# Three of each unit's 64 row maxima on ScalarE and GpSimd, in a fused attention and feed-forward kernel on one core

## The chip, the cores and the metric

The kernel runs on one core of one Trainium2 chip. The metric is the device time of one execution in microseconds (us), lower is better. Engines: TensorE (PE, and PEld for its weight loads), VectorE (DVE), ScalarE (ACT), GpSimd (POOL) and SyncE (SP, which here only issues DMAs). GpSimd issues DMAs too, in the order of its own program.

## The reference

One transformer block on x of shape 1 x 2048 x 512 in float32: a modulated layer norm, softmax attention with 32 heads of 16, and a SwiGLU feed-forward of width 1792.

```python
mod = (_silu(c) @ w_mod).reshape(c.shape[0], 6, 1, -1)
h = _layernorm(x) * (1 + ca) + sa
# in _A_ref: scores = q k^T / 4;  p = softmax(scores);  o = p v;  o @ wo
x = x + ga * _A_ref(h, A_wqkv, A_wo)
h = _layernorm(x) * (1 + cb) + sb
# in _B_ref: (silu(h @ w_gate) * (h @ w_up)) @ w_down
x = x + gb * _B_ref(h, B_w_gate, B_w_up, B_w_down)
```

## The kernel before, in words

**Units.** The attention is cut into 32 units: 4 chunks of 512 queries by 8 groups of 4 heads. A unit has 16 steps, one for each 128 keys. In a step TensorE makes four score tiles (`score`, L569), ScalarE takes their exponentials out of PSUM (L571), and `pv_step` multiplies them with the values (L584).

**Maxima.** The exponentials need each row's maximum over all 2048 keys, which is made ahead: `max_one(r)` multiplies 128 queries with 512 keys into a PSUM bank (L521), and VectorE reduces the 512 columns to one maximum a row (L523). A unit has 64 of them, four in a step, and they run LEAD = 21 steps ahead of the scores. When a unit's last one is issued, `max_rows` reduces the four maxima of a row to one (L528, VectorE), and the result is turned by TensorE (L533 to L535) and stored in two further rows of the unit's query tile `qop`, so that the score matmul subtracts it. The maxima use banks 0 to 3 in turn (`four`), the scores three others (`bank`).

**Order.** Everything is issued in an order written by hand; each engine follows its own part of it. `plain` runs windows of three pairs of one score and one maximum, and after each window one or two halves of a `pv_step`. The first `plain` stretch is 147 steps long (STARTS), attention alone; units 2 to 8 have their maxima in it. After it, feed-forward work of the finished chunk is mixed in.

**What else is in that stretch.** `split_weights` splits the feed-forward weights in two parts on GpSimd (L646, L647, L684) and stores them to DRAM (L650): three steps of it in each unit, about 3, 5 and 8 steps after a unit's scores begin. `close_unit(u)` runs when the values of unit u are done: the loads of the keys `kop` (three tiles in rotation) and queries `qop` for unit u + 3 (`load_k`, `load_q`; SP issues one half of the rows and GpSimd the other, L445), and, some steps later, the division: the denominators go to DRAM (L595, L600), come back broadcast as `rb` (L605), and GpSimd multiplies (`out_c`, L611) and stores (L612). In the order of GpSimd's program a unit of this stretch is so: loads for a coming unit, two weight steps, the multiplication at L611, the third weight step.

`tmp(name)` gives one of four 128 x 512 tiles in rotation, which the feed-forward uses too.

Of the kernel before, what the change touches and what calls it, by code (L numbers as in the profile page):

```python
# [14 lines left out]
ALU = mybir.AluOpType  # L15
AX = mybir.AxisListType
# [12 lines left out]
CW = S // NC  # L29
NG = H // 4  # L30
# [9 lines left out]
WIN = 3  # L40
HALVES = (2, 1, 1, 2)
ORDER = (0, 2, 1, 3)
UG = 16 * NG
PTS = 13
FBANKS = (3, 6)
# [56 lines left out]
def block_kernel(ctx, tc, x, wqkv, wo, w_gate, w_up, w_down, c, w_mod, out):  # L102
    nc = tc.nc
# [389 lines left out]
    qop, mx, pts, pv, o_, due, res = {}, {}, {}, {}, {}, {}, {}  # L493
# [12 lines left out]
    def load_q(u):  # L506
        ci, g = divmod(u, NG)
        qop[u] = pb.tile([P, 2, CW], F32R, name="qop", tag="qop", bufs=3)
        first, second = [(nc.gpsimd, nc.sync)[k] for k in ((0, 0), (1, 1), (1, 0))[min(u, 1) + (u > 2)]]
        load_parts(qop[u], qd, g, ci * CW, (ci + 1) * CW, second, first)  # L510

    def max_one(r):

        u, t = divmod(r // 4, 16)
        b, e = 1 - r % 4 // 2, r % 2
        s, qt, kc = t // 4 % 2, t % 4, t // 8 * 2 + e
        if u not in mx:
            mx[u] = pb.tile([P, 2, 2, 4, NC], F32, name="mx", tag="mx", bufs=3)
        rows = slice(64 * b, 64 * b + KR)
        pm = four("pm")  # L520
        nc.tensor.matmul(pm, qop[u][rows, s, qt * P:(qt + 1) * P], kop[u % 3][rows, s, kc * CW:(kc + 1) * CW],  # L521
                         start=True, stop=True)
        nc.vector.tensor_reduce(mx[u][:, b, s, qt, kc:kc + 1], pm, op=ALU.max, axis=AX.X)  # L523

    def max_rows(u):

# [36 lines left out]
    def score(i, h):  # L563
        u, kt = divmod(i, 16)
        rows = slice(64 * (h % 2), 64 * (h % 2) + KR + 2)
        p_ = pb.tile([P, CW], F32, name="pt_", tag="pt", bufs=PTS)
        pts.setdefault(i, {})[h] = p_
        sp = bank("st_")
        nc.tensor.matmul(sp, kop[u % 3][rows, h // 2, kt * P:(kt + 1) * P], qop[u][rows, h // 2, :],  # L569
                         start=True, stop=True)  # L570
        nc.scalar.activation(p_, sp, AF.Exp, scale=SCALE)  # L571
# [42 lines left out]
    def at(i, f):  # L614
        due.setdefault(i, []).append(f)
# [16 lines left out]
    def tmp(name):  # L632
        return pf.tile([P, CW], F32, name=name, tag="tmp", bufs=4)
# [261 lines left out]
    def begin(ci):  # L895
        x2 = pf.tile([P, 4, D], F32, name="x2", tag="x2", bufs=1)
        act = [pf.tile([P, NK, CW], F32R, name=f"act{a}", tag=f"act{a}", bufs=1) for a in range(2)]
        hT = [pf.tile([P, NK, CW], F32R, name=f"act{a}", tag=f"act{a}", bufs=1) for a in range(2)]
        chunks[ci] = ch = Chunk(ci, x2, act, hT)
        ch.load_x2(nc.sync if ci else nc.gpsimd)  # L900
# [43 lines left out]
    at(3, lambda: begin(0))  # L944
    at(UG - 2, lambda: chunks[0].load_wo())

# [3 lines left out]
    def after(i):  # L950
# [9 lines left out]
        if i == -2:  # L960
# [8 lines left out]
            load_q(2)  # L969
        if 0 <= i < UG and i % 16 in ((1, 4) if i < 16 else (3, 5, 8) if i < UG - 16 else (1, 3, 5)):  # L970
            next(weights2, None)
# [5 lines left out]
    def pair_of():  # L977
        nonlocal done
        i = done // 4 - 1
        most = 4 * n - 4 * (LEAD - 1)  # L980
        h = (ORDER if done < most else (0, 1, 2, 3))[done % 4]
        work = [lambda: score(i + 1, h)]
        if done < most:
            work.insert(1 - h % 2, lambda: max_one(done + 4 * (LEAD - 1)))
        for f in work:
            f()
        done += 1
        if side:
            side.pop(0)()

    for i in range(-LEAD, -1):
        if i == -LEAD + 3:
            load_k(1)
            load_q(1)
        for k, r in enumerate((0, 2, 1, 3)):
            max_one(4 * (i + LEAD) + r)
            if (4 * (i + LEAD) + k) % 6 == 1:
                take(late, 12 if i > -LEAD else 4)
        if i == -2:
            four, work = three, bank  # L1000
            for k in range(4):
                bank = Turn(7, 3, 6)
                for _ in range(WIN):
                    pair_of()
                bank = work
                if k < 3:
                    take(late, (9, 9, 8)[k])
        after(i)
        while side:
            side.pop(0)()  # L1010
# [174 lines left out]
```

## Time and profile before

| | |
|---|---|
| median of 3 runs | 1828.58 us (1827.91 to 1830.11) |
| span of the profiled execution | 1827.6 us |
| busy in that span | PE 99%, DVE 83%, ACT 69%, POOL 25% |
| the maxima on VectorE (L523) | 2048, 1274.3 us busy |
| chain that ended last | PE 82%, DVE 14% of the span |

The profile is of one execution of its own, whose time is its span; the runs are timed apart from it, and their median is 1.0 us over that span. Times in rows of order are microseconds from the span's start. In those rows stand the start, the duration, the engine, the line of the kernel, the operation, what it writes and reads, how often, and in brackets how long the engine had been idle and what ended that. A POOL or SP row with DMA in its name is the issue of a transfer, not the transfer.

### The profile page before, as it was taken

What the parts mean: (1) busy time and instruction counts of PE and PEld (TensorE: products, weight loads), DVE (VectorE), ACT (ScalarE), POOL (GpSimd) and SP (SyncE); (2) the same over time, 40 slices, a digit from 0 to 9 for tenths busy, and PEclk for the clock granted to TensorE, in tenths of its full rate; (3) what the DMA queues carried; (4) which work ended last, traced back from release to release, by engine and by line L of the source; (5) the groups of instructions that cost most, each with busy time, mean ns of one, the idle gap of its engine ahead of it and who ended that gap; (6) DMA issues with size and microseconds to landing.
All of it is one profiled execution on the core that took longest, in us unless ns stands there. A gap on an engine that the chain in (4) does not pass through costs nothing.

```text
span 1827.6 us, 41072 instructions
## 1 busy us (share of the span) xinstructions
PE 1818.3 (99%) x16904; PEld 1199.7 (66%) x16904; DVE 1523.2 (83%) x2554; ACT 1255.7 (69%) x2434; POOL 459.9 (25%) x538
## 2 busy tenths in 40 slices
PE   9999999999999999999999999999999999999999
PEld 7876444444455777776565777776464577767887
DVE  5578999999999888889999888889999988821544
ACT  4223888888888776777888777777888877774211
POOL 3612544556223111111123111111113011130200
PEclk9999999999999999999999999999999999999999
DMA  9884876667845454453544554444643536333742
GB/s 306 288 225 143 202 195 178 178 167 200 206 81 125 103 123 142 114 148 71 144 110 107 139 125 119 124 115 91 160 79 57 119 89 162 130 119 120 276 167 110
DMA packets 80488, 267.63 MB, mean 146 GB/s; under 512 B 19604, under 2 KB 24212, under 8 KB 59620
## 3 DMA queue, kind: packets, MB, share of 16 engines
q1 hardware_dynamic: 61324, 179.71, 34.1%
q0 software_dynamic: 18288, 84.49, 19.4%
q8 instruction: 133, 2.18, 0.5%
q10 hardware_dynamic: 688, 0.80, 0.2%
q14 instruction: 55, 0.45, 0.1%
HBM read 201.85 MB, written 62.13 MB: 144 GB/s over the span
## 4 chain that ended last, share of the span: by engine, by line
PE 82%; DVE 14%; ACT 1%; DMA 1%; issue 0%; SPq 0%; DVEq 0%; ACTq 0%
PE bank L584 21%; PE bank L786 20%; PE bank L569 14%; DVE mx L523 14%; PE bank L521 11%; PE bank L211 7%; PE bank L796 7%; DMA wm_ab<-in_w_mod 1%; PE bank L770 0%; DMA kop<-o_dr 0%; PE bank L163 0%; DMA rb<-d_dr 0%; ACT sq L820 0%; PE bank L839 0%; DVE v_flat L870 0%
## 5 line engine op out<-in xcount | busy, mean ns | idle before, releaser
L523 DVE TENSOR_REDUCE mx<-bank 128x1 f32<-128x512 f32 x2048 | 1274.3, 686 | 108.3 <-PE bank L521 54.6
L569 PE MATMUL bank<-qop,kop 50*128 50x512 f32 x2048 | 728.6, 425 | 0.4 <-ACT pt__16523 L571 0.2
L521 PE MATMUL bank<-kop,qop 48*128 48x512 f32 x2048 | 725.1, 425 | 0.3
L569 PEld LDWEIGHTS bank<-qop,kop 50*128 50x128 f32 x2048 | 343.6, 184 | 167.9 <-issue 49.7
L521 PEld LDWEIGHTS bank<-kop,qop 48*128 48x128 f32 x2048 | 344.0, 185 | 107.0 <-DVE mx L523 62.3
L786 PE MATMUL bank<-act,wgu 64*128 64x512 f32 x1872 | 301.4, 392 | 0.0
L786 PEld LDWEIGHTS bank<-act,wgu 64*128 64x128 f32 x1872 | 197.1, 187 | 24.3
L611 POOL TENSOR_TENSOR on<-o,rb 128x512 f32<-128x512 f32 x31 | 39.8, 1285 | 506.3 <-DMA rb<-d_dr 358.9
L786 PE MATMUL bank<-wd,mid 64*128 64x512 f32 x912 | 134.1, 397 | 0.1
L858 POOL CAST mid<-m 128x512 fp32r<-128x512 f32 x40 | 24.3, 607 | 380.9 <-DVE m L856 180.2
L786 PEld LDWEIGHTS bank<-wd,mid 64*128 64x128 f32 x912 | 88.3, 186 | 15.5 <-ACT first L893 3.2
L211 PE MATMUL bank<-hT,wqs 128*128 128x512 f32 x384 | 94.4, 397 | 0.4 <-DVE wqs L351 0.4
L854 DVE SCALAR_TENSOR_TENSOR q<-th,bank 128x512 f32<-128x512 f32 x56 | 38.2, 683 | 54.3 <-ACT th L850 54.3
L211 PEld LDWEIGHTS bank<-hT,wqs 128*128 128x128 f32 x384 | 70.7, 188 | 18.8 <-issue 2.9
L850 ACT ACTIVATE th<-bank 128x512 f32<-128x512 f32 x56 | 33.3, 594 | 57.9 <-PE bank L796 57.9
L870 DVE TENSOR_TENSOR x<-bank,x 128x512 f32<-128x512 f32 x84 | 53.9, 685 | 19.0 <-PE bank L786 16.8
L856 DVE TENSOR_TENSOR m<-bank,q 128x512 f32<-128x512 f32 x56 | 38.7, 692 | 21.7 <-PE bank L796 19.7
L859 POOL TENSOR_TENSOR mid<-m,mid 128x512 fp32r<-128x512 f32 x40 | 51.6, 1289 | 3.3
L796 PE MATMUL bank<-wd,mid 128*128 128x512 f32 x216 | 51.5, 394 | 0.0
L211 PE MATMUL bank<-wqs,hT 128*128 128x512 f32 x192 | 48.1, 398 | 0.0
L786 PE MATMUL bank<-wgu,act 64*128 64x512 f32 x288 | 47.0, 393 | 0.0
L796 PEld LDWEIGHTS bank<-wd,mid 128*128 128x128 f32 x216 | 40.4, 188 | 9.0 <-POOL mid L859 0.2
(6301 smaller groups left out, 5148.9 us busy)
## 6 DMA issues: line engine op xcount, KB each, us to landing
wgu<-gu_dr SPq DMA_DIRECT2D x48, 1024.0 KB
wd<-wd_dr SPq DMA_DIRECT2D x28, 1024.0 KB
kop<-kd SPq DMA_DIRECT2D x33, 768.0 KB
kop<-kd POOLq DMA_DIRECT2D x29, 768.0 KB, 8.7
gu_dr<-wgu POOLq DMA_DIRECT2D x14, 1024.0 KB, 13.6
kd<-prt SPq DMA_DIRECT2D x16, 512.0 KB
qd<-prt SPq DMA_DIRECT2D x16, 512.0 KB
kop<-gu_dr SPq DMA_DIRECT2D x8, 1024.0 KB
```

The lines of the kernel that those rows point to most:

```text
L211: nc.tensor.matmul(pt, lhs(a, k), rhs(b, k), start=(n == 0), stop=(n == 3 * nk - 1))
L521: nc.tensor.matmul(pm, qop[u][rows, s, qt * P:(qt + 1) * P], kop[u % 3][rows, s, kc * CW:(kc + 1) * CW], start=True, stop=True)
L523: nc.vector.tensor_reduce(mx[u][:, b, s, qt, kc:kc + 1], pm, op=ALU.max, axis=AX.X)
L569: nc.tensor.matmul(sp, kop[u % 3][rows, h // 2, kt * P:(kt + 1) * P], qop[u][rows, h // 2, :], start=True, stop=True)
L584: nc.tensor.matmul(pv[u][32 * h:32 * h + 32, cols], v_flat[:, e0:e0 + 32], p_[h][:, cols], start=(kt == 0 and half == 0), stop=(kt == 15), ...
L611: mul.tensor_mul(on, o, rb)
L786: nc.tensor.matmul(outs[e], lhs(e, a, k)[rows], rhs(b, k)[rows], start=(ph == 0 and j == 0), stop=(j == z and (ph == 1 or trade is not None)),
L796: nc.tensor.matmul(outs[e], lhs(e, a, k), rhs(b, k), start=(j == 0), stop=(j == z))
L854: nc.vector.scalar_tensor_tensor(q, th, 1.0, outs[0], op0=ALU.add, op1=ALU.mult)
L856: nc.vector.tensor_mul(m32, outs[1], q)
L859: (nc.gpsimd if slow else nc.vector).tensor_sub(mid[:, 1, :], m32, mid[:, 0, :].bitcast(F32))
L870: nc.vector.tensor_add(ch.x2[:, t, :], outs[e], ch.x2[:, t, :])
```

## The change

In units 2 to 8 the maxima number 0, 6 and 12 of the 64 are not reduced by VectorE. ScalarE copies their PSUM bank into a `tmp` tile ("far"), and after the third copy is issued, GpSimd takes the maxima: `max_apart` halves the width again and again, each time as b + max(a - b, 0) in three operations: each tile for itself down to 64 columns, the three together from there to two, and then the last pair. Its scratch is a fourth `tmp` tile ("near"). The results go where VectorE would have put them.

```diff
+APART = (0, 6, 12)
...
-        nc.vector.tensor_reduce(mx[u][:, b, s, qt, kc:kc + 1], pm, op=ALU.max, axis=AX.X)
+        place = mx[u][:, b, s, qt, kc:kc + 1]
+        if 2 <= u <= NG and r % 64 in APART:
+            apart.append((tmp("far"), place))
+            nc.scalar.copy(apart[-1][0], pm)
+            if len(apart) == len(APART):
+                max_apart()
+        else:
+            nc.vector.tensor_reduce(place, pm, op=ALU.max, axis=AX.X)
+
+    apart = []
+
+    def larger(out, a, b, d):
+        nc.gpsimd.tensor_sub(d, a, b)
+        nc.gpsimd.tensor_scalar_max(d, d, 0.0)
+        nc.gpsimd.tensor_add(out, b, d)
+
+    def max_apart():
+
+        k, w = len(apart), CW // 8
+        d = tmp("near")
+        few = d[:, CW // 2:CW // 2 + k * w].rearrange("p (k w) -> p k w", k=k)
+        for j, (far, _) in enumerate(apart):
+            for v in (4 * w, 2 * w, w):
+                larger(few[:, j, :] if v == w else far[:, 0:v], far[:, 0:v], far[:, v:2 * v], d[:, 0:v])
+        while w > 2:
+            w //= 2
+            larger(few[:, :, 0:w], few[:, :, 0:w], few[:, :, w:2 * w],
+                   d[:, 0:k * w].rearrange("p (k w) -> p k w", k=k))
+        nc.gpsimd.tensor_sub(d[:, 0:k], few[:, :, 0], few[:, :, 1])
+        nc.gpsimd.tensor_scalar_max(d[:, 0:k], d[:, 0:k], 0.0)
+        for j in range(k):
+            nc.gpsimd.tensor_add(apart.pop(0)[1], few[:, j, 1:2], d[:, j:j + 1])
```

## The prediction

> **What bounds the kernel now.** I read the page's first part, then the chain of work that ended last in the stretch where the changed units lie, then busy times by unit, then VectorE's and GpSimd's rows in order of time.
>
> ```profile
> span 1827.6 us, 41072 instructions
> PE 1818.3 (99%) x16904; PEld 1199.7 (66%) x16904; DVE 1523.2 (83%) x2554; ACT 1255.7 (69%) x2434; POOL 459.9 (25%) x538
> ...
> 242.63 26.92 DVE mx L523 x46
> ...
> core 0: us, PE busy (x) PEld busy (x) DVE busy (x) ACT busy (x) POOL busy (x), PEclk, DMA share, GB/s
> 242.00:280.00 38.00, 38.00 (x392) 18.42 (x390) 38.00 (x66) 33.26 (x66) 20.09 (x21) 1.00 0.72 188
> ...
> 242.42 0.22 DVE L528 TENSOR_REDUCE m<-mx 128x16 f32<-128x64 f32 x1
> 242.54 28.79 DVE L523 TENSOR_REDUCE mx<-bank 128x1 f32<-128x512 f32 x48
> ...
> 474.30 0.21 DVE L528 TENSOR_REDUCE m<-mx 128x16 f32<-128x64 f32 x1
> ```
>
> The reduction of L528 closes a unit's maxima, so its rows mark the units: unit 2's at 242.42 us, unit 8's at 474.30, six units of 38.65 us on average between them. The changed units 2 to 8 therefore lie between about 202 and 474 us. There the chain runs along VectorE's maxima (46 in a row), which follow each other every 0.60 us (48 in 28.79), without a gap. So VectorE paces this stretch; TensorE's queue is as full, ScalarE is at 88% and GpSimd at 53%. By these shares alone the change looks right: it takes work from the engine that paces to the one that is half idle.
>
> But GpSimd's half idle time is not free time of any kind: where in its order the new work lands decides. Its rows, first by unit, then around one place:
>
> ```profile
> 241.67 1.28 POOL L611 TENSOR_TENSOR on<-o,rb 128x512 f32<-128x512 f32 x1 [17.21 <-ACT pt__2307 L571]
> ...
> 282.55 1.27 POOL L611 TENSOR_TENSOR on<-o,rb 128x512 f32<-128x512 f32 x1 [18.48 <-DMA rb<-d_dr]
> ...
> 322.36 1.28 POOL L611 TENSOR_TENSOR on<-o,rb 128x512 f32<-128x512 f32 x1 [17.44 <-DMA rb<-d_dr]
> ...
> 360.23 1.26 POOL L611 TENSOR_TENSOR on<-o,rb 128x512 f32<-128x512 f32 x1 [15.24 <-DMA rb<-d_dr]
> ...
> 250.88 0.58 POOL L650 DMA_DIRECT2D wd_dr<-wd  x1 [0.30 <-POOL wd L647]
> 251.46 0.58 POOL L445 DMA_DIRECT2D kop<-kd  x1
> 252.03 0.58 POOL L445 DMA_DIRECT2D qop<-qd  x1
> ...
> 263.48 0.59 POOL L650 DMA_DIRECT2D gu_dr<-wgu  x1 [0.30 <-POOL wgu L647]
> ```
>
> All of GpSimd's idle time in a unit is one wait, at L611, for a row of denominators that comes when its unit ends. From one L611 to the next, without that wait, GpSimd needs 282.55 - 241.67 - 18.48 = 22.4 us (22.4 and 22.6 for the next two). Its slack is 38.65 - 22.4 = 16.2 us a unit. That is the number to hold against the change.
>
> **The change, part by part.** (1) VectorE loses 3 of 64 maxima in each of 7 units: 3 x 0.60 = 1.8 us a unit, 12.6 us in all, on the path as long as nothing else takes its place.
>
> (2) ScalarE gains 3 copies of 128x512 from PSUM a unit. The row of such a copy in this stretch:
>
> ```profile
> L588 ACT COPY o<-bank x6: 585/588/612, 214.8 to 408.3; 128x512 f32<-128x512 f32 x6
> ```
>
> That is 1.8 us a unit, against 4.7 us that ScalarE is idle in the 38 us of the table. They come within 13 of a unit's 64 steps, between the exponentials, and can hold a score bank some tenths of a us longer; between 0 and 1.8 us a unit. I take nothing, because they are covered if (3) is right; if it is wrong they eat part of (1).
>
> (3) GpSimd gains one call of `max_apart` a unit. Each of the three tiles goes through widths 256, 128 and 64 with three operations each (27), all three together through 32, 16, 8, 4 and 2, that is 96, 48, 24, 12 and 6 elements a partition (15), and then two operations and three adds (5): 47 instructions, nearly all waiting for the one before. The rows nearest to them:
>
> ```profile
> 565.11 0.20 POOL L753 TENSOR_TENSOR rs<-rs,mv 128x4 f32<-128x4 f32 x1
> 565.40 0.20 POOL L754 TENSOR_SCALAR rs<-rs 128x4 f32<-128x4 f32 x1
> ...
> 567.08 0.20 POOL L756 TENSOR_TENSOR rs<-mv,rs 128x4 f32<-128x4 f32 x1
> 567.38 0.77 POOL L765 TENSOR_SCALAR mid<-x,rs,rs 128x512 f32<-128x512 f32 x1
> ...
> L647 POOL TENSOR_TENSOR wgu<-mid,wgu 128x512 fp32r<-128x512 f32 x28 | 35.8, 1280 | 2.3
> L647 POOL TENSOR_TENSOR wd<-mid,wd 128x1024 fp32r<-128x1024 f32 x7 | 16.7, 2387 | 0.6
> L646 POOL CAST wgu<-mid 128x512 fp32r<-128x512 f32 x28 | 17.3, 618 | 0.0
> ```
>
> From 565.11 to 567.08 seven dependent operations of 4 elements take 1.97 us: 0.28 us each from start to start, though each lasts 0.20. The fixed part is 47 x 0.28 = 13.2 us. Two-input operations cost (2387 - 1280)/512 = 2.16 ns an element: 3 x 2 x 448 + 2 x 186 = 3060 elements, 6.6 us. One-input operations cost (772 - 197)/508 = 1.13 ns by L765 and L754 (0.8 by the cast): 3 x 448 + 186 = 1530 elements, 1.7 us. Less 0.3 us for the four elements that are in the fixed part: 21.2 us a call. This is 5 us over the slack of 16.2. The change spends most of GpSimd's time not on elements but on starting instructions.
>
> Here a rule bears on the row. The Trainium skill, Perfetto Trace Analysis, section GPSIMD Engine Instruction, holds that GpSimd spans don't add up and are to be timed by the spacing of consecutive starts. The spacing of 0.28 us against spans of 0.20 agrees with it. By spans alone the call would be 47 x 0.20 + 8.0 = 17.4 us, still over the slack.
>
> (4) What is queued behind it. In program order the call comes when the third tile is copied, at the unit's 13th maximum; that is after the weight step that ends with the store at 250.88 us, and before the load of the next unit's keys and queries at 251.46. Each queue: on POOL the load of `kop` and `qop` for unit u+1 (half the rows; SP issues the other half unmoved) stands behind the call for unit u. No transfer is added. How long these loads take, and when they are needed:
>
> ```profile
> kop<-kd POOLq DMA_DIRECT2D x1, 768.0 KB, 8.3
> ...
> kop<-kd POOLq DMA_DIRECT2D x1, 768.0 KB, 15.7
> ...
> qop<-qd POOLq DMA_DIRECT2D x1, 192.0 KB, 8.8
> ...
> 278.26 0.40 PE L521 MATMUL bank<-kop,qop 48*128 48x512 f32 x1
> ...
> 471.69 0.39 PE L521 MATMUL bank<-kop,qop 48*128 48x512 f32 x1
> ```
>
> The rows of 8.3 and 8.8 us are the load for unit 3, with nothing ahead of it in the queue (the load for unit 5, behind a 1 MB store, took 15.7; after 21 us of arithmetic that store has left). `qop` lands 0.57 + 8.8 = 9.4 us after the `kop` issue. The two matmuls are the first maxima of unit 4 (the 257th of L521) and of unit 9 (the 577th). They read the rows that POOL loads, and TensorE takes its work in order: if these are late, the exponentials and the values behind them are late too.
>
> A second rule, for the landing: the Trainium skill, DMA: Bandwidth & Descriptors, section on the SWDGE (gpsimd) path, gives 2.0 us and bytes over 436e3, an estimate of 3.8 us for 768 KB. The row has 8.3, so the measurement decides; by the rule the sum below would be 4.5 us less.
>
> **The sum.** The rows for the start and the end of the stretch:
>
> ```profile
> 203.02 0.60 POOL L650 DMA_DIRECT2D wo_dr<-wgu  x1 [0.30 <-POOL wgu L647]
> 211.65 0.57 POOL L445 DMA_DIRECT2D kop<-kd  x1 [8.03 <-PE bank L521]
> ...
> 223.87 0.59 POOL L650 DMA_DIRECT2D gu_dr<-wgu  x1 [0.30 <-POOL wgu L647]
> ...
> 507.00 1.28 POOL L611 TENSOR_TENSOR on<-o,rb 128x512 f32<-128x512 f32 x1 [23.89 <-ACT pt__5723 L571]
> ```
>
> Unit 2's call finds GpSimd idle (its wait of 8.0 us ends at 211.65), runs from 203.6 to 224.8, and its load lands at 234, before unit 3 starts near 240; the weight work (12.8 us, from 211.65 to the end of the store of 223.87) then ends before the L611 at 241.67. Covered. Unit 3's call starts at 251.46 and ends at 272.7; the load lands at 282.1 instead of serving at 278.26: 3.8 us late. From there GpSimd has no wait left: 12.6 us of weight work (251.46 to 264.07) bring it to 285, past 282.55 when the denominators come, and the next call follows. Its period is 22.4 + 21.2 = 43.6 us, against 38.65. The load for unit 9 then lands at 251.46 + 21.2 + 5 x 43.6 + 9.4 = 500.1, 28.4 us after 471.69. VectorE's relief is worth nothing in a stretch paced by GpSimd; at most unit 2's 1.8 us ahead of it would be kept, and I take none. Behind unit 8 there are no more calls, GpSimd gets its waits back (23.9 us at the L611 of 507.00) and the lateness stays as it is. 1827.6 + 28.4 = 1856.0 us of span; the median of the runs is 1.0 us over the profiled span, so 1857.0.
>
> Both ends of the unknown cost: 17.4 us a call (spans without the spacing) gives a period of 39.8 and 28.4 - 6 x 3.8 = 5.6 us, 1834; one-input operations at the worst row of that kind, below, 2.8 ns an element, give 23.8 us a call and 28.4 + 6 x 2.6 = 44 us, 1873. I stay at the chained rows, the nearest in kind.
>
> ```profile
> L265 POOL TENSOR_SCALAR minus<-ident 128x128 f32<-128x128 f32 x1 | 0.5, 548 | 0.1
> ```
>
> **The rivals.** (a) Faster: GpSimd keeps up and VectorE's relief counts. It decides at a call of 16.2 us or less, which would take 47 instructions at 0.17 us fixed; no row is that short. Then up to 12.6 us come off, but TensorE is also full and ScalarE's copies crowd the same 13 steps, so about half: 1822. Chance 0.07. (b) Nothing: the calls fit or nearly fit, and what VectorE gives up TensorE takes over as pace, which the full PE column speaks for and the spacing row against: 1828, chance 0.04. (c) Slower, but by ScalarE: the copies hold score banks and VectorE's reduction waits for GpSimd's result; 7 x 1.8 us at most, 1841, while GpSimd holds its loads in time. Nothing shows this stronger than (3); chance 0.04. (d) My forecast, 1857, chance 0.85; between its ends it may lie from 1834 to 1873.
>
> **How the numbers follow.** 0.2% of this kernel is 3.7 us, about what a measurement can tell from no change. Faster 0.07 from (a), same 0.04 from (b), slower 0.89 from (c) and (d). The range 1838 to 1870 leaves out (a) and (b), and the outer tips of (d), 2 in 10 together.
>
> **What would show it.** Right: no wait left at L611 from the second call on; POOL near full from 251 us on; the loads of L445 on POOL some 20 us later against the unit's start than now; a wait of TensorE for `kop` or `qop` of some 4 to 5 us once in each of units 4 to 9; L528 rows 43 to 44 us apart there and 38 before and after; VectorE with gaps. Wrong: a call much under 21 us, L611 still waiting, or L528 rows 36 to 38 us apart, which would be (a).

## The result: slower by 3.1%, and the profile after

| | before | after |
|---|---|---|
| median of the runs | 1829.25 us (4 runs, 1827.91 to 1830.11) | 1886.0 us (4 runs, 1883.17 to 1886.64) |
| ratio to before | | 1.0307 [1.0295, 1.0319] |
| span of the profiled execution | 1827.6 us | 1883.9 us |

The forecast was 1857.0 us, from 1838 to 1870: right in direction, 28.4 us expected and 56.3 us found between the two profiled spans. Where they arose is seen in the time at which each unit's first maximum reaches TensorE (rows of the line that multiplies for the maxima, L521 before and L522 after; us from the span's start):

| unit | 3 | 4 | 5 | 6 | 7 | 8 | 9 | 10 |
|---|---|---|---|---|---|---|---|---|
| before | 239.8 | 278.3 | 317.1 | 355.8 | 394.2 | 433.1 | 471.7 | 510.1 |
| after | 239.0 | 289.5 | 337.0 | 380.4 | 431.2 | 477.4 | 525.9 | 567.4 |
| late by | -0.8 | 11.2 | 19.9 | 24.6 | 37.0 | 44.3 | 54.2 | 57.3 |

Until unit 3 nothing is lost. From unit 4 on every unit is late by 5 to 12 us more, and after unit 10 it stays.

In the changed kernel the line numbers are shifted: L522 is the multiplication for a maximum, L531 VectorE's reduction, L536, L537 and L538 the subtraction, the max with 0 and the addition of a halving, L446 the loads of `kop` and `qop`, L637 the load of `rb`, L643 the multiplication that was L611. The page of the changed kernel, its first lines, the row of the granted clock in 40 slices, and the shares of the chain that ended last:

```profile
span 1883.9 us, 41445 instructions
PE 1834.6 (97%) x16904; PEld 1200.5 (64%) x16904; DVE 1516.4 (80%) x2533; ACT 1266.1 (67%) x2455; POOL 596.0 (32%) x867
...
PEclk9999998898989999999999999999999999999999
...
PE 85%; POOL 4%; DVE 4%; DMA 3%; ACT 2%; issue 1%; SPq 0%; POOLq 0%; DVEq 0%
```

Over the whole span GpSimd is busy only a third of the time, so the first part of the page alone would not convict it. But DVE's share of the chain has fallen from 14% to 4%, and POOL and DMA have 7% together, where everything beside PE and DVE had 4%. GpSimd's rows in order of time, changed kernel, in the first three changed units, then the two later waits for `rb` and the load for unit 9 (start, duration, engine, line, operation):

```profile
203.09 0.75 POOL L536 TENSOR_TENSOR near<-far 128x256 f32<-128x256 f32 x1
...
226.24 0.64 POOL L446 DMA_DIRECT2D kop<-kd  x1
...
246.59 1.29 POOL L643 TENSOR_TENSOR on<-o,rb 128x512 f32<-128x512 f32 x1 [7.57 <-ACT pt__2431 L603]
...
256.40 0.75 POOL L536 TENSOR_TENSOR near<-far 128x256 f32<-128x256 f32 x1
...
279.54 0.64 POOL L446 DMA_DIRECT2D kop<-kd  x1
280.18 0.58 POOL L446 DMA_DIRECT2D qop<-qd  x1
...
292.17 1.29 POOL L643 TENSOR_TENSOR on<-o,rb 128x512 f32<-128x512 f32 x1
...
325.17 0.64 POOL L446 DMA_DIRECT2D kop<-kd  x1
...
388.52 1.28 POOL L643 TENSOR_TENSOR on<-o,rb 128x512 f32<-128x512 f32 x1 [5.15 <-DMA rb<-d_dr]
...
483.44 1.26 POOL L643 TENSOR_TENSOR on<-o,rb 128x512 f32<-128x512 f32 x1 [3.76 <-DMA rb<-d_dr]
...
516.37 0.64 POOL L446 DMA_DIRECT2D kop<-kd  x1
```

A call lasts from the first row of L536 to the issue of `kop`: 226.24 - 203.09 = 23.15 us, 279.54 - 256.40 = 23.14. The load for unit 4 is issued at 279.54, where it was issued at 251.46 before, and unit 4 needed it at 278.26. Between 279.54 and 325.17 GpSimd has no wait worth a row: 45.6 us is its own program, one call in it. Two later periods hold a wait for `rb`, and the first L643 comes late (246.59, before 241.67).

What TensorE does meanwhile: the waits of the changed kernel, all engines, 200 to 560 us (total, times, longest), and two steps of the chain in the same stretch:

```profile
DVE mx L531 <- PE bank L522: 45.5, 18, 12.9
PE bank L522 <- DMA qop<-qd: 37.7, 5, 11.0
...
POOL on L643 <- DMA rb<-d_dr: 8.9, 2, 5.1
```

```profile
280.18 9.14 DMA qop<-qd
...
325.80 11.08 DMA qop<-qd
```

TensorE, in whose order the unit's first maximum comes next, stands still for the query rows, five times in 37.7 us, and VectorE behind it. VectorE's own rows in order of time, changed kernel, show that it has nothing to do then, and that while it has work it is as fast as before:

```profile
279.76 0.22 DVE L560 TENSOR_REDUCE m<-mx 128x16 f32<-128x64 f32 x1
292.88 3.08 DVE L531 TENSOR_REDUCE mx<-bank 128x1 f32<-128x512 f32 x5 [12.90 <-PE bank L522]
...
300.83 21.61 DVE L531 TENSOR_REDUCE mx<-bank 128x1 f32<-128x512 f32 x36 [0.64 <-PE bank L601]
```

36 maxima in 21.61 us are 0.60 us each, with GpSimd's halvings running from 302.00 on beside them. So GpSimd's halvings do not slow VectorE; VectorE waits for TensorE, TensorE for a load, the load for GpSimd.

### The profile page after: what moved, and what is told of

Its sections match the earlier page's. It is cut to its first block, busy times and chain, and to the rows that moved or that the text cites. A ratio compares the mean times of both kernels' runs of the same rounds, so it can differ in the third digit from the quotient of the medians.

```text
span 1883.9 us, 41445 instructions
## 1 busy us (share of the span) xinstructions
PE 1834.6 (97%) x16904; PEld 1200.5 (64%) x16904; DVE 1516.4 (80%) x2533; ACT 1266.1 (67%) x2455; POOL 596.0 (32%) x867
## 4 chain that ended last, share of the span: by engine, by line
PE 85%; POOL 4%; DVE 4%; DMA 3%; ACT 2%; issue 1%; SPq 0%; POOLq 0%; DVEq 0%
PE bank L616 23%; PE bank L818 19%; PE bank L601 15%; PE bank L522 12%; PE bank L828 8%; PE bank L212 7%; DVE mx L531 4%; DMA qop<-qd 2%; POOL near L537 1%; POOL near L536 1%; PE bank L871 1%; PE bank L802 0%; DMA wm_ab<-in_w_mod 0%; POOL far L538 0%; DMA qop<-mr 0%
## 5 line engine op out<-in xcount | busy, mean ns | idle before, releaser
L531 DVE TENSOR_REDUCE mx<-bank 128x1 f32<-128x512 f32 x2027 | 1265.1, 682 | 175.0 <-PE bank L522 110.7
L522 PE MATMUL bank<-kop,qop 48*128 48x512 f32 x2048 | 730.8, 428 | 39.0 <-DMA qop<-qd 37.7
L601 PE MATMUL bank<-qop,kop 50*128 50x512 f32 x2048 | 738.1, 429 | 2.7 <-DMA qop<-mr 0.9
L522 PEld LDWEIGHTS bank<-kop,qop 48*128 48x128 f32 x2048 | 345.5, 186 | 147.4 <-issue 60.0
L643 POOL TENSOR_TENSOR on<-o,rb 128x512 f32<-128x512 f32 x31 | 39.9, 1288 | 420.3 <-DMA rb<-d_dr 234.0
L902 DVE TENSOR_TENSOR x<-bank,x 128x512 f32<-128x512 f32 x84 | 53.9, 685 | 18.3 <-PE bank L818 16.8
L888 DVE TENSOR_TENSOR m<-bank,q 128x512 f32<-128x512 f32 x56 | 38.7, 692 | 21.7 <-PE bank L828 19.7
L537 POOL TENSOR_SCALAR near<-near 128x256 f32<-128x256 f32 (+4 forms) x98 | 47.1, 481 | 8.6
```

Source lines behind the costliest of these rows:

```text
L531: nc.vector.tensor_reduce(place, pm, op=ALU.max, axis=AX.X)
L537: nc.gpsimd.tensor_scalar_max(d, d, 0.0)
L643: mul.tensor_mul(on, o, rb)
L888: nc.vector.tensor_mul(m32, outs[1], q)
L902: nc.vector.tensor_add(ch.x2[:, t, :], outs[e], ch.x2[:, t, :])
```

## The experiments

The theory (G in the expectations): GpSimd's program with the call in it is longer than a unit, and the loads that stand behind the call make TensorE late. The rivals: ScalarE's copies do it (S), or only the place of the call in GpSimd's order does it. After the first runs a part was added: what GpSimd's DMA queue carries, moved by the call (the load, and the loads and stores of weights that follow it), meets `rb` and holds it up. Lines and ratios are against the kernel before on the same chip; edits are against the changed kernel.

**One maximum, or two, instead of three** (fewer instructions on GpSimd, fewer copies).

```diff
-APART = (0, 6, 12)
+APART = (0,)        # e1_one
+APART = (0, 6)      # e2_two
```

> One maximum a unit goes to GpSimd instead of three (APART holds 0 alone). Theory G (GpSimd's whole program sets the pace: its own 22.4 us a unit plus the call, and the load of the next unit's keys stands behind the call): a call is 5.6 us for the tile by the rows of the changed kernel, about 4.6 for the fifteen small operations and 0.9 for the end, 11 us, under the slack of 16.2. The load then lands near 272 us, before unit 4 needs it at 278. No stall; at most 7 x 0.6 = 4.2 us gained: 1825 to 1829. Rival S (the copies on ScalarE, in order between the exponentials, hold the score banks): the loss goes with the number of copies, a third of 57 us: about 1848.

> Two maxima a unit go to GpSimd (0 and 6). G: a call is 11.1 us for the tiles, about 5 for the small operations and 1.1 for the end, 17.2 us, a little over the slack. Period 39.6 us against 38.65: about 1 us lost in each of six units, more if the denominators are late too: 1830 to 1845, I say 1836. S: two thirds of the loss, 1867.

One: 1837.64 us, ratio 1.0039 [1.0022, 1.0056]. Two: 1860.02 us, 1.0162 [1.0145, 1.0179]. Both miss what G said, from above, and S from below. GpSimd's rows in order of time with one maximum, then SP's issue of `rb` among them (L682 is the weight store that was L650):

```profile
263.71 0.65 POOL L446 DMA_DIRECT2D kop<-kd  x1 [0.33 <-PE bank L601]
...
275.81 0.58 POOL L682 DMA_DIRECT2D gu_dr<-wgu  x1 [0.30 <-POOL wgu L679]
...
283.59 1.28 POOL L643 TENSOR_TENSOR on<-o,rb 128x512 f32<-128x512 f32 x1 [7.19 <-DMA rb<-d_dr]
...
304.66 0.64 POOL L446 DMA_DIRECT2D kop<-kd  x1 [0.33 <-PE bank L616]
...
446.76 1.27 POOL L643 TENSOR_TENSOR on<-o,rb 128x512 f32<-128x512 f32 x1 [8.83 <-DMA rb<-d_dr]
```

```profile
277.08 0.57 SPq L637 DMA_DIRECT2D rb<-d_dr  x1
```

With one, GpSimd still waits 5 to 9 us a unit: it has time left, and yet time is lost. What it waits for is `rb`, issued by SP at 277.08 and 436.38: 6.5 and 10.4 us until L643, where it was about 5 before. The load of `kop` and `qop` is not what `rb` meets here, for it had landed at 273.2. It is the weight stores behind it (L682, issued at 272.95 and 275.81, landed at 279.3 and 281.8): from 278 to 280 us GpSimd's queue takes 82% of the DMA engines' time, and in the kernel before these stores had landed by 277.3, before `rb` left at 277.53. The wait moves the next call and so the next load. With two, the distances between `kop` issues are 45.2, 39.6, 46.8, 39.5, 45.9 us: 39.6 is what G had computed, and every second one is 6 to 7 us longer, by the wait for `rb`. So the size of the call is right, and a second thing stretches every period in which GpSimd would be in time.

**`rb` three steps earlier, with one maximum** (the reciprocal, its store and `rb` are issued earlier).

```diff
-APART = (0, 6, 12)
+APART = (0,)
...
-        at(i0 + 3, lambda: res.__setitem__(u, out_b(u, nc.sync, *res[u])))
-        at(i0 + 4, lambda: res.__setitem__(u, out_r(u, nc.sync, *res[u])))
+        e0 = i0 if 0 <= u <= 6 else i0 + 3
+        at(e0 + 0, lambda: res.__setitem__(u, out_b(u, nc.sync, *res[u])))
+        at(e0 + 1, lambda: res.__setitem__(u, out_r(u, nc.sync, *res[u])))
```

> One maximum a unit (as in the first experiment, which ended 0.39% slower), and the reciprocal and its two transfers three steps earlier for units 0 to 6. In the first experiment the call of 11.6 us fits, but the load, 11 us later, leaves with the transfer that L643 waits for (8 to 10 us instead of 5), and by units 8 and 9 the load itself was late. G with contention: with the transfer out of the way every load lands before its unit; left are the copies: 0 to 2 us over the run before, 1830 to 1832. Without that contention: as the first experiment, 7 us over the run before.

1828.61 us, 1.0000 [0.9991, 1.0009], against 1.0039 with `rb` at its old place, some 7 us less. GpSimd's rows of this run, then SP's issue of `rb` among them:

```profile
301.66 0.64 POOL L446 DMA_DIRECT2D kop<-kd  x1 [0.33 <-PE bank L601]
...
340.33 0.64 POOL L446 DMA_DIRECT2D kop<-kd  x1 [0.33 <-PE bank L616]
...
357.90 1.27 POOL L643 TENSOR_TENSOR on<-o,rb 128x512 f32<-128x512 f32 x1 [4.90 <-DMA rb<-d_dr]
```

```profile
341.28 0.57 SPq L637 DMA_DIRECT2D rb<-d_dr  x1
```

The loads are 38.7 us apart, a unit of before. So it was the late `rb` that made one maximum slow, and not the copy. The collision itself is still there: `rb` now leaves 1 us behind the `kop` load and takes 16.6 us until L643. But it leaves 14 us earlier than with one maximum alone (355.72), and so it is in time. All that is reached is the time before.

**The same with three maxima.**

```diff
-        at(i0 + 3, lambda: res.__setitem__(u, out_b(u, nc.sync, *res[u])))
-        at(i0 + 4, lambda: res.__setitem__(u, out_r(u, nc.sync, *res[u])))
+        e0 = i0 if 0 <= u <= 7 else i0 + 3
+        at(e0 + 0, lambda: res.__setitem__(u, out_b(u, nc.sync, *res[u])))
+        at(e0 + 1, lambda: res.__setitem__(u, out_r(u, nc.sync, *res[u])))
```

> The changed kernel, but for units 0 to 7 the reciprocal of the denominators and the two transfers behind it (L631, L632, L637) are issued three steps, about 7 us, earlier. G with contention: in the changed kernel the transfer that L643 waits for took 16 us in two of six units because it left with the load of keys and queries, and 8 in the first, against 5 before; that added 4.9, 5.1 and 3.8 us to three periods. Earlier, it is done before; every period is 45.6 us: 14 us less, 1872. Without that contention: no change, 1886.

1881.57 us, 1.0285 [1.0268, 1.0303]: more than expected. Up to unit 9 it went as expected; from the second call on `rb` leaves 6 to 10 us ahead of the load, and no wait for it is left there. The `kop` issues are now 45.5 us apart without exception (274.19, 319.69, 365.15, 410.65, 456.11, 501.62), and unit 9's first maximum comes at 511.4 instead of 525.9, 14.5 us earlier. Then most of it is given back: from unit 9 to unit 10 it takes 51.2 us and not 41.5. The waits and the chain of this run behind 505 us:

```profile
DVE dn L631 <- DMA dn<-o: 6.6, 1, 6.6
```

```profile
529.39 8.52 DMA dn<-o
```

The reciprocal of the denominators (L631) was moved ahead with the rest; its load lands late, and VectorE stands 6.6 us at it, of the 9.7 us that are given back, with maxima queued behind. The edit took away the waits for `rb` and made a new one.

**The call behind the loads** (the place in GpSimd's order).

```diff
-                max_apart()
+                at(16 * u - 14, max_apart)
```

> The change with its call put off by three to four steps, so that GpSimd issues the load of the next unit's keys and queries first and takes the maxima behind it. The rival by which the place in the queue is all: near the run before, with the copies' few us, 1830 to 1836. Theory G: GpSimd still needs 45.6 us a unit; the wait moves from TensorE's keys to VectorE's L560, which needs the call's results: unit 3's call ends near 283 us against 280, and each later unit 7 us later against its place: about 37 us by unit 8, 1866.

1871.73 us, 1.0233 [1.0216, 1.025]: near G's 1866, far from the rival's 1830 to 1836. The loads are early again (`kop` for unit 4 at 256.39 us), but they stay 45.5 us apart. The waits of this run from 205 to 530 us, among them:

```profile
DVE m L560 <- POOL mx L555: 29.1, 5, 7.5
```

Now the unit's last reduction waits for the three maxima themselves, 5 times. The place decides what waits, not whether something does.

**SP issues all loads of units 3 to 9**, so that none of them stands behind the call.

```diff
-        load_parts(kop[u % 3], kd, u % NG, 0, S, nc.gpsimd if u > 2 else nc.sync)
+        load_parts(kop[u % 3], kd, u % NG, 0, S, nc.gpsimd if u > 9 else nc.sync)
-        first, second = [(nc.gpsimd, nc.sync)[k] for k in ((0, 0), (1, 1), (1, 0))[min(u, 1) + (u > 2)]]
+        first, second = [(nc.gpsimd, nc.sync)[k] for k in ((0, 0), (1, 1), (1, 0))[min(u, 1) + (u > 9)]]
```

> The changed kernel, but for units 3 to 9 the half of the keys and queries that GpSimd loads is issued by SP, so nothing that TensorE reads for its maxima stands behind the call. G says that GpSimd is over its time (45.6 against 38.65 us a unit) whatever its order is: its results come later by 7 us more in each unit, and once they are later than the unit's last maximum, VectorE's L560 waits for them. The first units run free (28 us of slack between the third copy and L560), then the loss comes back: about 5 x 7 + 23 - 28 = 30 us slower than before, 1850 to 1865. A rival by which the place of the loads is all: at most 5 us from before, 1823 to 1834.

1859.37 us, 1.0163 [1.0134, 1.0192], as expected. GpSimd's rows and VectorE's, each in order of time:

```profile
286.72 1.30 POOL L643 TENSOR_TENSOR on<-o,rb 128x512 f32<-128x512 f32 x1
...
331.01 1.29 POOL L643 TENSOR_TENSOR on<-o,rb 128x512 f32<-128x512 f32 x1
```

```profile
363.87 0.22 DVE L560 TENSOR_REDUCE m<-mx 128x16 f32<-128x64 f32 x1 [4.82 <-POOL mx L555]
...
408.13 0.22 DVE L560 TENSOR_REDUCE m<-mx 128x16 f32<-128x64 f32 x1 [5.38 <-POOL mx L555]
```

GpSimd's period is 44.3 us without the two issues, and after some units at the old pace, in which it falls behind unseen, it passes 44.3 us a unit on to VectorE. It is the length of its program that binds.

**Other forms of the max with 0**, which are to change the length of the call alone (both places of the max are changed; the second is not shown). The third leaves the max out (times a 1 and plus a 0, both read from a column), the fourth too (times 1.0); in these two the exponent is scaled by 1/8, which alone costs nothing that shows: the fourth form has the price list of the change and its time.

```diff
-        nc.gpsimd.tensor_scalar_max(d, d, 0.0)
+        nc.gpsimd.tensor_scalar(d, d, 0.0, 0.0, op0=ALU.max, op1=ALU.add)                      # e3_imm2
+        nc.gpsimd.tensor_scalar(d, d, nil[:, 0:1], nil[:, 0:1], op0=ALU.max, op1=ALU.add)      # e4_ptr
+        nc.gpsimd.tensor_scalar(d, d, one[:, 0:1], nil[:, 0:1], op0=ALU.mult, op1=ALU.add)     # e9_mult_add
+        nc.gpsimd.tensor_scalar_mul(d, d, 1.0)                                                 # e10_mult
```

> All three maxima as in the change, but each max with zero is a two-operation instruction (max with 0, then add 0, both immediate) in place of the one-operation form. In the changed kernel the one-operation max took 0.85 us for 256 elements, 2.6 ns an element, as the first one-operation scalar instruction of the kernel before did (548 ns for 128), while two-operation scalar instructions there took 1.13 ns. If the price belongs to the one-operation form: 1.4 ns x 1530 elements = 2.2 us off each call, six periods shorter by that, about 13 us: 1873. If it belongs to the operation max: no change, 1886. Under S: no change, too.

> The same with both operands of the two operations taken from a column of zeros in SBUF (max with it, then add it), the form whose rows gave 1.13 ns an element. If the price belongs to immediates or to the one-operation form: 2.2 us off each call, 1873. If it belongs to max: 1886.

> The changed kernel with each max with zero replaced by times one, plus zero, both from columns in SBUF: the operations of the rows that the prediction took its 1.13 ns an element from (L765). The maximum is left out by that (the result is the first of the two numbers), and the exponent is scaled by an eighth. If that rate belongs to multiply and add, and max is dearer whatever its form: 256 elements take about 0.48 us instead of 0.85, a call is 2.2 us shorter or a little more, six periods: 12 to 15 us faster than the change, about 1872. If the rate of small pieces is 2.6 ns in any case: 1886.

> The same with times one alone, immediate, the one-operation form (maximum left out, exponent scaled by an eighth). The first such instruction of the kernel before took 548 ns for 128 elements. If one-operation immediates cost that: 0.53 us for 128 and 0.85 for 256 as max does, time as the change, 1886. If max itself is the price: near 0.48 us for 256, 1872.

| form | ratio to before | 256 elements | GpSimd's undisturbed period |
|---|---|---|---|
| as changed | 1.0307 [1.0295, 1.0319] | 0.847 us | 45.6 us |
| max and add, immediate | 1.0335 [1.0313, 1.0356] | 1.071 us | 47.0 us |
| max and add, from a column | 1.0415 [1.0395, 1.0434] | 1.224 us | 49.5 us |
| mult and add, from columns | 1.0313 [1.0293, 1.0334] | 0.554 us | 45.2 us |
| mult, immediate | 1.0304 [1.0284, 1.0325] | 0.850 us | 45.6 us |

The first two were meant to make the call shorter and made it longer; as doses of GpSimd time they serve all the same, for the time of the kernel rises with the period, while VectorE's and ScalarE's work is the same. They are not clean doses: in the second, after the first L643, GpSimd has no wait for `rb` left, where the changed kernel has 8.9 us. The last two tell what the price hangs on; the third was expected 12 to 15 us faster than the change and is not. The groups by shape of the changed kernel, then of the third and of the fourth form (count, busy us, mean ns):

```profile
L537 POOL TENSOR_SCALAR near<-near 128x256 f32<-128x256 f32 x21 | 17.8, 847 | 1.9
L536 POOL TENSOR_TENSOR near<-far 128x256 f32<-128x256 f32 x21 | 15.6, 741 | 1.2
L537 POOL TENSOR_SCALAR near<-near 128x128 f32<-128x128 f32 x21 | 11.1, 526 | 1.8
L536 POOL TENSOR_TENSOR near<-far 128x128 f32<-128x128 f32 x21 | 9.7, 460 | 1.6
```

```profile
L537 POOL TENSOR_SCALAR near<-near,one,nil 128x256 f32<-128x256 f32 x21 | 11.6, 554 | 2.2
L537 POOL TENSOR_SCALAR near<-near,one,nil 128x128 f32<-128x128 f32 x21 | 9.4, 448 | 2.2
L537 POOL TENSOR_SCALAR near<-near,one,nil 128x6 f32<-128x6 f32 x7 | 2.6, 367 | 0.7
```

```profile
L537 POOL TENSOR_SCALAR near<-near 128x256 f32<-128x256 f32 x21 | 17.8, 850 | 1.9
L537 POOL TENSOR_SCALAR near<-near 128x128 f32<-128x128 f32 x21 | 11.1, 530 | 1.8
```

A multiplication by an immediate costs what the max costs: (847 - 526)/128 = 2.5 ns an element and 0.2 us fixed. Multiplication and addition from columns cost (554 - 448)/128 = 0.8 ns an element, but 0.36 us fixed (by the row of 6 elements). So the one-input operation with an immediate is dearer per element than the two-input subtraction ((741 - 460)/128 = 2.2 ns), for both operations that were tried. The cheap form saves at 256 and loses at the small widths, 0.4 us a call in all.

**The copies alone, and the relief alone.** In the first the copies stay and GpSimd only takes the first column of each, no maximum; in the second there are no copies either, and a constant stands for the three maxima. In both the exponent is scaled by 1/8.

```diff
+        while apart:                                     # e5_copies, for the whole of max_apart
+            far, place = apart.pop(0)
+            nc.gpsimd.tensor_copy(place, far[:, 0:1])
...
+            nc.gpsimd.memset(place, -1000.0)             # e6_relief, for the copies and the call
...
-        nc.scalar.activation(p_, sp, AF.Exp, scale=SCALE)
+        nc.scalar.activation(p_, sp, AF.Exp, scale=SCALE / 8)   # both
```

> VectorE's relief and ScalarE's copies as in the change, but GpSimd takes no maximum: it copies the first column of each tile to the place (three small operations a unit, under 1 us). Left out: the maximum over the other 511 columns in those places, and the exponent is scaled by an eighth so that it stays finite. Theory G: nothing is behind a long call any more, the loss is gone, and what is left is what the relief is worth with the copies: between 12.6 us faster (all of it) and 0, I say 4 to 6 faster, 1824. Rival S (copies on ScalarE cost the time): most of the loss stays, over 1860.

> The same without the copies: the three banks are not read at all and GpSimd sets their places to -1000 (those three maxima are left out, and the exponent is scaled by an eighth). It gives the relief of VectorE alone. G: 1816 to 1824; against the run before it shows what ScalarE's copies take. If both are equal the copies are covered; if this one is faster by more than 2 us they are not.

Copies alone: 1831.76 us, 1.0014 [1.0005, 1.0024]. Relief alone: 1827.97 us, 0.9987 [0.9978, 0.9996]. The loss is gone with the call, as G has it and against S. But both gains expected were too large: 4 to 6 us with the copies, and 1816 to 1824 us without; taking 21 maxima off VectorE for nothing brings 2 us. Busy times of the relief alone from 242 to 280 us (PE, PEld, DVE, ACT, POOL, then granted clock), and by line its chain from 242 to 434 us, then that of the kernel before in the same stretch:

```profile
242.00:280.00 38.00, 38.00 (x390) 18.37 (x392) 36.73 (x63) 33.19 (x66) 20.08 (x24) 1.00 0.72 186
```

```profile
by line: PE bank L613 43.8%; PE bank L598 27.8%; PE bank L522 27.4%; PE bank L564 0.6%; PE bank L563 0.5%; PE bank L562 0.0%; issue 0.0%
```

```profile
by line: DVE mx L523 95.3%; issue 1.8%; PE bank L584 1.0%; PE bank L521 0.6%; DVE m L528 0.5%; DVE dn L599 0.4%; PE bank L569 0.3%; PE bank L535 0.1%; PE bank L534 0.1%; DVEq L528 0.0%; PE bank L533 0.0%
```

Before, the chain was VectorE's maxima to 95%; with three of 64 gone it is TensorE's matmuls altogether, and VectorE is free for 1.3 of 38 us. TensorE was right behind. The copies take back 1831.76 - 1827.97 = 3.8 us. So ScalarE's part (S) is real but small, 4 us where no call covers it, against the 57 of the change, and even a GpSimd that kept up would leave nothing of the gain.

No version beat the kernel before: the best that computes the maxima equals it, and what the relief alone gains is smaller than the copies cost.

## Why the prediction was right and where it was wrong

**Right: what binds.** Step (4) and the sum's build held: the load for the next unit stands behind the call, TensorE waits for its query rows, VectorE gets gaps, the lateness begins with unit 4, grows with each of units 4 to 9 and then stays. GpSimd's period without a wait was 45.6 us, which is the predicted 22.4 and the call that was measured, 23.15. (TensorE's waits for the load were expected as 4 to 5 us in each of units 4 to 9; they were 3.1 to 11.0 us in five of these. The load of 15.7 us that step (4) gives to unit 5 is the one for unit 6, issued at 332.16; the sum does not use it.) Experiments with the call put elsewhere, with the loads put elsewhere, and with dearer forms of it all followed this period.

**Right: the landing.** 9.4 us were taken from the `kop` issue to the landing of `qop`; 280.18 + 9.14 - 279.54 = 9.8 us was measured for unit 4 and 9.5 for unit 9 (516.37 to 525.9). The rule of the Trainium skill that was weighed there (DMA: Bandwidth & Descriptors, the section on the SWDGE path) would have had it 4.5 us shorter; the trace does not agree with it here.

**Wrong: the size of the call, step (3).** 21.2 us was predicted, 23.15 measured. The 32 two-input operations were right: 12.6 us of spans against 13.0. The 15 one-input operations last 7.0 us against 15 x 0.20 + 1.7 = 4.7. The term that failed is the 1.13 ns an element: it took its fixed part from an operation with two immediates (L754) and its long one from an operation with two column operands (L765), and neither is the form of the halving. That form, one immediate, has 0.2 us and 2.5 ns an element; the column form has 0.36 us and 0.8 ns. The row of the right form was the one of L265, 548 ns for 128 elements, which stood in the prediction as the far end. Six calls up to unit 9's load: 6 x 1.95 = 11.7 us.

**Wrong: that unit 2's call is covered, and that GpSimd has no wait left at L611 from unit 3's call on.** The sum let `rb` land when it had landed before. It came late three times that counted: 246.59 instead of 241.67 at the first L643 (4.9 us), 5.15 and 3.76 us of waits at 388.52 and 483.44. That is 13.8 us. (The row of 246.59 names an instruction of ScalarE as what ended its wait. I put it down to `rb`, which SP issued at 238.33, 1.9 us later than before: with `rb` three steps earlier the same L643 starts at 241.34, and its row names `rb`.) What meets `rb` is GpSimd's own DMA traffic, moved by the call. In the first case the load had landed at 235.8, and it is the weight stores behind it, issued at 235.60 and 238.45; in the other two the load itself leaves at the same time as `rb`. When SP issued `rb`, changed kernel:

```profile
238.33 0.57 SPq L637 DMA_DIRECT2D rb<-d_dr  x1
...
372.28 0.57 SPq L637 DMA_DIRECT2D rb<-d_dr  x1
...
467.52 0.56 SPq L637 DMA_DIRECT2D rb<-d_dr  x1
```

From 238.33 to the start of L643 it is 8.3 us, from 372.28 and 467.52 it is 16, where the kernel before took about 5 (issued at 236.42, used at 241.67). GpSimd's load for the next unit had been issued at 370.69 and 467.02. The DMA queues of the changed kernel from 372 to 376 us, then from 376 to 380 (packets, MB, share of the 16 engines' time):

```profile
q0 software_dynamic: 89, 0.73, 106.9%
```

```profile
q0 software_dynamic: 158, 0.54, 89.0%
```

GpSimd's own queue is the only one in these 8 us and holds nearly all the time of the 16 DMA engines, though 0.73 MB in 4 us are only 182 GB/s; `rb` has none of them. The hardware queue's first packets come between 380 and 384 us. The Trainium skill (DMA: Bandwidth & Descriptors, section Queues, rings and completion order) has each engine take turns between its queues packet by packet; by that `rb` should have had packets in the first 8 us, and this trace does not show it. Why it had none, no run here tells. That the late `rb` costs this time is shown by the two runs that issue it earlier: some 7 us less with one maximum, 14.5 us at unit 9 with three. That the collision makes it late is read from these rows; no run tests it by itself.

**The account.** At unit 9 the kernel is 54.2 us late: 28.4 predicted, 11.7 from the call, 13.8 from `rb`, 53.9 together. From unit 9 to 10 another 3.1 us are lost (41.5 us instead of 38.4), for which the prediction had no term. The last of TensorE's stalls, and its clock (the third column from the right) around it, changed kernel:

```profile
525.91 0.76 PE L522 MATMUL bank<-kop,qop 48*128 48x512 f32 x1 [6.65 <-DMA qop<-qd]
```

```profile
518.00:526.00 8.00, 1.35 (x14) 0.54 (x13) 2.36 (x4) 2.04 (x4) 7.38 (x10) 0.75 0.95 161
526.00:536.00 10.00, 10.00 (x77) 4.42 (x79) 6.41 (x12) 5.26 (x12) 9.21 (x7) 0.69 0.63 263
```

The granted clock is 0.69 on average in the 10 us after the restart (0.50 in the first five, 0.88 in the second): 10 x 0.31 = 3.1 us of TensorE's work. Most of the loss is this: in the run that multiplies by an immediate, TensorE waited only 0.8 us for unit 9's load, the clock stayed at 1.00, and unit 9 to unit 10 took 39.3 us. The clock falls after each of the five stalls (the shortest 3.1 us), but between units 4 and 9 GpSimd sets the pace and it costs nothing there: with `rb` early the `kop` issues were 45.5 us apart although the stalls were there. The Trainium skill (TensorE: Matmul & The Clock Gate, section What's actually happening) has the clock at half after an idle window of some 3.4 us and full again after a busy one of the same length, in windows whose start does not follow the work; 0.31 x 10 / 0.5 = 6.2 us at half clock after the restart agrees with that, one window and up to another for its start.

**Step (1) and the rival (a).** "12.6 us off as long as nothing else takes its place" was the right caveat with too high a price: the relief is worth 2 us (0.9987 [0.9978, 0.9996]), because TensorE, busy in all 38 of 38 us, was level with VectorE. Rival (a) had halved the sum to about 6 us; with the copies at 3.8 us it was in truth no gain at all. **Step (2)** took the copies at nothing, with 0 to 1.8 us a unit as bounds; 3.8 us over 7 units is 0.5 us a unit, inside these. Neither shows in the result, since GpSimd covers both.

**The range.** It ended at 1870 because the high end of (d), 1873, came from the dearer row of one price alone. The wait for `rb` was not a bound that was too low but a term that was missing.

## What to carry to other kernels

The slack of a half idle engine is the length of a unit less its own program (here 38.65 - 22.4 = 16.2 us, against a call of 23.15), and work that is put into its order also moves the DMAs issued behind it: look up which transfers these then meet, and who waits for those. Price an operation by a row of the same form of operands, not merely of the same engine. And before work is taken off the engine that paces, leave it out altogether in a trial: here that showed a ceiling of 2 us, less than the copies cost.

## What the runs showed of the hardware

On GpSimd the one-input operation with an immediate (max or mult) took 0.85 us for 128x256 float32, longer than the two-input subtraction (0.74 us); max and add with two immediates took 1.07 us; max and add from a column 1.22 us; mult and add from columns only 0.55 us, but 0.37 us at 6 elements, where the immediate one takes 0.23 to 0.25. While GpSimd's own DMA queue kept the DMA engines full, a 256 KB load issued by SP went from about 5 us to 16. And VectorE's maxima kept 0.60 us each while GpSimd ran its halvings.
